# Splitting one input load by tokens and re-dealing the last output stores over three DMA-issuing engines

**Chip, cores, metric.** One core of one Trainium2 chip. The metric is the device time of one execution in microseconds (us), the median of several runs. A DMA has "landed" when the last of its 16 semaphore counts is in the trace.

## The reference, cut to what matters

Linear attention over 8 batches and 8 heads, followed by a two-layer network with SiLU on all 4608 tokens:

```python
q_s, k_s = softmax(q, axis=-1), softmax(k, axis=2)        # (8, 8, 576, 64)
kv = np.einsum('bhsd,bhse->bhde', k_s, v)
x = np.einsum('bhsd,bhde->bhse', q_s, kv)                 # to (4608, 512)
h = x @ w_in                                              # (512, 2048)
return (h * (1 / (1 + np.exp(-h))) @ w_out)               # (2048, 512), float32
```

## The kernel before

The parts that the argument touches. `nc.sync` is SP, `nc.scalar` ACT, `nc.vector` DVE, `nc.gpsimd` GpSimd (POOL in the profile), `nc.tensor` PE (PEld is its weight load). A q behind an engine's name (SPq, POOLq) means its instruction queue. The order of the calls is the order in each engine's queue.

```python
def load(b, name, src, cc, eng):                 # half a batch: 576 KB, one DMA
    t = ld.tile([128, 2, J * D], FP32, name=name)
    st[b][name, cc] = t
    x = src[b].rearrange("(g r) (p j) d -> g (r p) (j d)", r=2, j=J)
    eng.dma_start(out=t, in_=x.rearrange("g x y -> x g y")[:, 2 * cc:2 * cc + 2, :])

def vcast(b, cc, eng, g0=0, g1=2):               # v to bf16, by pairs of heads
    o = vaug[:, :, 2 * cc + g0:2 * cc + g1, 0:D]
    i = jgd(b, "vt", cc)[:, :, g0:g1, :]
    copy(eng, o, i)

# ... the start, batch 0
load(0, "vt", v, 0, nc.sync)
load(0, "kt", k, 1, nc.sync)
load(0, "vt", v, 1, nc.sync)
# ...
xt_mm(0, 0, 320, 256, 0, 0)
heat(3, 6)                                       # three warm-up matmuls of 512 columns
vcast(0, 1, nc.scalar, 0, 1)
vcast(0, 1, nc.vector, 1, 2)
trcopy(0, 1, 0, 5, 2, nc.scalar)
trcopy(0, 1, 5, J, 3)
kv(0, 1)                                         # the k-v product: 36 matmuls, 64 rows
# ... the middle: what is planned for one chunk t, by unit number
for i in range(2):
    # ...
    plan(u + (2, 11)[i], lambda i=i: vcast(b, i, nc.gpsimd))
# ... the end: one tile of the output
def part(name, bank, th, n, a):
    o = w_out_tile(last, th)[:, a, n * HN:(n + 1) * HN]
    nc.vector.scalar_tensor_tensor(out=o, in0=PS[...], scalar=OS, in1=WG[...], ...)
    one, two = {
        (0, 0): (nc.sync, nc.sync),
        (1, 1): (nc.gpsimd, nc.gpsimd),
        (1, 0): (nc.scalar, nc.sync),
        (0, 1): (nc.scalar, nc.gpsimd) if a == 0 else (nc.sync, nc.scalar),
    }[th, n]
    for i, eng in enumerate((one, two)):         # two stores of 64 KB
        eng.dma_start(out=rows(...), in_=o[i * P:(i + 1) * P, :])
```

The softmax here doesn't subtract the row's maximum and nothing guards it: scores larger than these inputs give would overflow.

## Time and profile before

| | |
|---|---|
| time, 3 runs | 263.25 us median (262.77 to 263.55) |
| span of the profiled run | 260.8 us, granted clock 1.000 |
| first wide matmul starts | 15.26 us |
| last arithmetic (DVE) ends | 256.90 us |
| last store lands | 259.62 us |
| from last arithmetic to the end | 3.90 us |

The rows are points on one time axis, from the first to the last instruction. The change works ahead of the second row and behind the fourth. The lines that show this are in the prediction.

### The profile page before, as it was taken

To read this page: it belongs to the slowest core of one execution; us is meant where nothing else is said; L and a number is where in the kernel's file an instruction comes from. 1 tells how busy PE (TensorE), PEld (TensorE's weight loads), DVE (VectorE), ACT (ScalarE), POOL (GpSimd) and SP (SyncE) were. 2 spreads that over 40 slices of the span, in tenths; PEclk is the share of its full clock that TensorE was granted. 3 is DMA by queue.
4 is the path that set the end of the run, shared out by engine and by line. 5 is a ranking of instruction groups with operands and counts; after the bars stand their busy time and mean duration, and the time that the engine had idled before them with its cause. 6 is when DMAs were issued, how large, how long until landed. Compare 5 with 4: busy or idle time off the path is not lost.

```text
span 260.8 us, 6412 instructions
## 1 busy us (share of the span) xinstructions
PE 252.4 (97%) x2732; PEld 203.0 (78%) x2732; DVE 207.3 (79%) x268; ACT 187.6 (72%) x212; POOL 66.9 (26%) x62
## 2 busy tenths in 40 slices
PE   8799999999999999999999999999999999999993
PEld 3457756656887888888888888888888888888882
DVE  2967786879997999799979997999798548855832
ACT  5767877998994799579956996699664757584710
POOL 1753691741360306030603060306000000000004
PEclk9999999999999999999999999999999999999999
DMA  7999999689979477957784879640424002500534
GB/s 248 334 198 298 298 323 333 253 186 384 309 284 222 123 209 247 197 146 201 258 220 118 214 249 152 182 104 3 90 61 102 3 0 46 117 3 1 120 84 121
DMA packets 35452, 45.89 MB, mean 176 GB/s; under 512 B 16208, under 2 KB 19984, under 8 KB 35424
## 3 DMA queue, kind: packets, MB, share of 16 engines
q1 hardware_dynamic: 29488, 33.63, 47.2%
q0 software_dynamic: 5616, 11.60, 16.9%
q8 instruction: 21, 0.34, 0.5%
q10 hardware_dynamic: 320, 0.26, 0.4%
q14 instruction: 7, 0.06, 0.1%
HBM read 36.70 MB, written 9.44 MB: 177 GB/s over the span
## 4 chain that ended last, share of the span: by engine, by line
PE 80%; DVE 12%; ACT 2%; POOL 2%; DMA 1%; issue 1%; POOLq 0%; DVEq 0%; ACTq 0%
PE PS L468 34%; PE PS L368 32%; PE PS L405 5%; PE PS L258 3%; PE PS L228 2%; DVE zq L148 2%; PE PS L189 2%; DVE h L346 2%; DMA qt<-in_q_dram 1%; PE PS L276 1%; DVE eq L157 1%; DVE GT L442 1%; DVE S L442 1%; ACT eq L108 1%; POOL out_dram L730 1%
## 5 line engine op out<-in xcount | busy, mean ns | idle before, releaser
L346 DVE TENSOR_TENSOR h<-PS,h 128x1024 f32<-128x1024 f32 (+1 forms) x45 | 53.9, 1199 | 12.0 <-PE PS L368 6.0
L468 PEld LDWEIGHTS <-GT 128*128 128x128 f16 x512 | 49.5, 98 | 6.9 <-issue 1.2
L368 PEld LDWEIGHTS <-WS 128*128 128x128 f16 x480 | 46.8, 98 | 7.5 <-issue 1.4
L468 PE MATMUL PS<-W,GT 128*128 128x256 f16 x384 | 49.1, 273 | 0.0
L368 PE MATMUL PS<-XS,WS 128*128 128x256 f16 (+1 forms) x360 | 46.3, 272 | 0.6 <-DVE h L346 0.5
L352 ACT ACTIVATE GT<-h 128x1024 f16<-128x1024 f32 (+1 forms) x45 | 46.1, 1047 | 0.3 <-DVE h L346 0.3
L89 ACT COPY h<-PS 128x1024 f32<-128x1024 f32 (+1 forms) x35 | 35.1, 1003 | 13.9 <-PE PS L368 13.4
L157 POOL TENSOR_TENSOR eq<-eq,rzq 128x1152 bf16<-128x1152 bf16 x13 | 27.7, 2134 | 57.6 <-DVE rzq L152 56.1
L468 PEld LDWEIGHTS <-S 128*128 128x128 f16 x384 | 37.1, 98 | 5.5 <-issue 1.0
L368 PEld LDWEIGHTS <-W 128*128 128x128 f16 x360 | 34.7, 98 | 4.8 <-issue 0.5
L468 PE MATMUL PS<-T,S 128*128 128x256 f16 x256 | 32.7, 273 | 0.1
L368 PE MATMUL PS<-XT,W 128*128 128x256 f16 (+1 forms) x240 | 29.5, 272 | 0.1
L352 ACT ACTIVATE GT<-PS 128x1024 f16<-128x1024 f32 (+1 forms) x15 | 15.2, 1016 | 18.9 <-PE PS L368 18.9
L91 POOL CAST vaug<-vt 128x1152 bf16<-128x1152 f32 x12 | 15.8, 1322 | 43.3 <-DMA vt<-in_v_dram 41.1
L730 POOL DMA_DIRECT2D out_dram<-ow x5 | 2.7, 546 | 72.1 <-DVE ow L715 72.1
L108 ACT ACTIVATE eq<-qt 128x1152 bf16<-128x1152 f32 (+1 forms) x18 | 19.0, 1057 | 2.5 <-DMA qt<-in_q_dram 2.4
L113 ACT ACTIVATE ek<-kt 128x1152 bf16<-128x1152 f32 x16 | 18.4, 1153 | 1.2 <-DMA kt<-in_k_dram 1.2
L148 DVE TENSOR_REDUCE zq<-eq 128x18 f32<-128x1152 bf16 x12 | 16.1, 1344 | 3.8 <-ACT eq L108 3.8
L258 PE MATMUL PS<-XT,W 128*128 128x288 f16 x128 | 16.3, 286 | 0.5 <-DVE XT L91 0.2
L468 PE MATMUL PS<-W,S 128*128 128x256 f16 x128 | 16.5, 273 | 0.0
L488 DVE SCALAR_TENSOR_TENSOR ow<-PS,sc 128x512 f32<-128x512 f32 x7 | 4.8, 691 | 14.4 <-ACT sc L484 14.4
L258 PEld LDWEIGHTS <-W 128*128 128x128 f16 x128 | 12.4, 98 | 4.3 <-issue 1.3
(78 smaller groups left out, 346.0 us busy)
## 6 DMA issues: line engine op xcount, KB each, us to landing
out_dram<-ow SPq DMA_DIRECT2D x64, 128.0 KB, 2.4
qt<-in_q_dram SPq DMA_DIRECT2D x12, 576.0 KB, 4.4
kt<-in_k_dram SPq DMA_DIRECT2D x12, 576.0 KB, 5.5
vt<-in_v_dram SPq DMA_DIRECT2D x12, 576.0 KB, 5.4
qt<-in_q_dram POOLq DMA_DIRECT2D x4, 576.0 KB, 10.3
kt<-in_k_dram POOLq DMA_DIRECT2D x4, 576.0 KB, 13.9
vt<-in_v_dram POOLq DMA_DIRECT2D x4, 576.0 KB, 13.2
W<-in_moe_w_out_dram POOLq DMA_DIRECT2D x4, 512.0 KB, 15.0
```

What stands on the lines that cost most here:

```text
L89: eng.copy(out=o, in_=i)
L91: eng.tensor_copy(o, i)
L108: nc.scalar.activation(out=half(st[b]["eq"], cc)[:, :, g0:g1], in_=jgd(b, "qt", cc)[:, :, g0:g1], func=ACT.Exp)
L113: nc.scalar.activation(out=half(ek, cc), in_=jgd(b, "kt", cc), func=ACT.Exp)
L148: nc.vector.reduce_sum(out=z, in_=e, axis=AX.X)
L157: eng.tensor_tensor(out=e, in0=e, in1=r[:, :, :, None].to_broadcast([128, J, 2, D]), op=ALU.mult)
L258: nc.tensor.matmul(out=PS[:, 2 * (fb % 3) + n, 0:S // 2], lhsT=W1[:, c, fb * 128:(fb + 1) * 128], rhs=XTS[0][:, c, n * (S // 2):(n + 1) * ...
L346: nc.vector.tensor_tensor(out=four(t, i), in0=group_bank(t, True), in1=four(t, i), op=ALU.add)
L352: nc.scalar.activation(out=group_out(t, f, n), in_=x, func=ACT.Silu, scale=1.0 / XS)
L368: nc.tensor.matmul(out=PS[:, bank + p // 2, (p % 2) * HT:(p % 2) * HT + width(t)], lhsT=a[:, c, p * 128:(p + 1) * 128], rhs=bb[:, c, 0:wid ...
L405: nc.tensor.matmul(out=PS[:, 2 + tb, :], lhsT=GTS[t % 2][:, fc, tb * 128:(tb + 1) * 128], rhs=W2[:, fc, :], start=(fc == 0), stop=(fc == N ...
L468: nc.tensor.matmul(out=PS[:, bank, m * HN:(m + 1) * HN], lhsT=a[:, fc, m * 128:(m + 1) * 128], rhs=bb[:, fc, :], start=(first and fc == 0) ...
```

## The change

Its intent: (1) the second half of batch 0's v comes in two pieces of tokens, so that one engine can cast the first piece while the second still arrives; (2) no engine issues more than two of the last stores in a row, so that the last ones don't queue up behind an issue.

```diff
-    def load(b, name, src, cc, eng):
+    def load(b, name, src, cc, eng, js=(0, J)):
...
-        eng.dma_start(out=t, in_=x.rearrange("g x y -> x g y")[:, 2 * cc:2 * cc + 2, :])
+        x = x.rearrange("g x y -> x g y")[:, 2 * cc:2 * cc + 2, :]
+        for j0, j1 in zip(js, js[1:]):
+            eng.dma_start(out=t[:, :, j0 * D:j1 * D], in_=x[:, :, j0 * D:j1 * D])
...
-    def vcast(b, cc, eng, g0=0, g1=2):
-        o = vaug[:, :, 2 * cc + g0:2 * cc + g1, 0:D]
-        i = jgd(b, "vt", cc)[:, :, g0:g1, :]
+    def vcast(b, cc, eng, g0=0, g1=2, j0=0, j1=J):
+        o = vaug[:, j0:j1, 2 * cc + g0:2 * cc + g1, 0:D]
+        i = jgd(b, "vt", cc)[:, j0:j1, g0:g1, :]
...
-    load(0, "vt", v, 1, nc.sync)
+    load(0, "vt", v, 1, nc.sync, (0, 5, J))
...
-    vcast(0, 1, nc.scalar, 0, 1)
-    vcast(0, 1, nc.vector, 1, 2)
+    vcast(0, 1, nc.vector, j1=5)
+    vcast(0, 1, nc.scalar, j0=5)
...
-            (0, 0): (nc.sync, nc.sync),
-            (1, 1): (nc.gpsimd, nc.gpsimd),
-            (1, 0): (nc.scalar, nc.sync),
-            (0, 1): (nc.scalar, nc.gpsimd) if a == 0 else (nc.sync, nc.scalar),
-        }[th, n]
+            (0, 0): ((nc.sync, nc.sync), (nc.sync, nc.sync)),
+            (1, 1): ((nc.sync, nc.sync), (nc.gpsimd, nc.gpsimd)),
+            (1, 0): ((nc.scalar, nc.scalar), (nc.gpsimd, nc.gpsimd)),
+            (0, 1): ((nc.sync, nc.scalar), (nc.sync, nc.gpsimd)),
+        }[th, n][a]
```

## The prediction

> **What bounds the kernel now.** I read the busy shares first, then the chain of waits near both edited places, then the timeline of those microseconds, then the DMA records. TensorE carries the kernel:
>
> ```profile
> PE 252.4 (97%) x2732; PEld 203.0 (78%) x2732; DVE 207.3 (79%) x268; ACT 187.6 (72%) x212; POOL 66.9 (26%) x62
> ```
>
> The change touches neither the matmuls nor anything between 15 and 250 us of the 260.8 us span. So the question is two small ones: does the first wide matmul (15.26 us) start earlier, and does the last store land earlier? Here is the chain of waits around the split load of v, then the timeline of the same stretch (start, length, both us):
>
> ```profile
> 12.36 0.44 PE PS L228 x8
> 12.80 0.76 PE PS L542 x3
> 13.55 0.45 PE PS L189 x32
> 14.02 0.18 DVE rz L200
> ...
> 12.65 0.68 ACT L89 CAST vaug<-vt 128x576 bf16<-128x576 f32 x1 [0.16 <-DMA vt<-in_v_dram]
> 12.65 0.76 DVE L91 CAST vaug<-vt 128x576 bf16<-128x576 f32 x1 [0.35 <-DMA vt<-in_v_dram]
> 12.73 0.82 PE L542 MATMUL PS<-XS 128*128 128x512 f16 x3
> 13.48 0.48 PE L189 MATMUL PS<-vaug,ek 64*64 64x65 bf16 x36
> ```
>
> Both casts really wait for the load. But the chain does not run through them: it runs through the three warm-up matmuls of L542 that stand ahead of the k-v product (L189) in TensorE's queue. I test that on the two other places where 64-row products follow 512-column matmuls:
>
> ```profile
> 9.18 1.67 PE L542 MATMUL PS<-XS 128*128 128x512 f16 x7
> 10.78 0.48 PEld L189 LDWEIGHTS <-ek 64*64 64x64 bf16 x36 [0.42 <-issue]
> ...
> 37.73 1.24 PE L405 MATMUL PS<-W,GT 128*128 128x512 f16 x5
> 38.90 0.29 PE L189 MATMUL PS<-vaug,ek 64*64 64x65 bf16 x12
> ```
>
> The product (or its weight load) starts 0.07 us before the recorded end of the last wide matmul in each: 10.85 - 10.78, 38.97 - 38.90, and in our place 13.55 - 13.48. The same offset three times, with different casts behind it, says that our product starts when TensorE lets it, not when the cast ends (13.41). The waits view names ACT vaug as its releaser with 0.4 us; I put that aside as the later of two releases only by the profile's bookkeeping, since the cast on DVE ended later still.
>
> At the end, stores issue from three queues; the last arithmetic is the DVE line:
>
> ```profile
> 254.39 2.70 POOL L730 DMA_DIRECT2D out_dram<-ow  x5 [72.14 <-DVE ow L715]
> 255.18 2.70 ACTq L730 DMA_DIRECT2D out_dram<-ow  x4
> 256.47 0.42 DVE L715 SCALAR_TENSOR_TENSOR ow<-PS,sb 128x256 f32<-128x256 f32 x1 [0.45 <-PE PS L468]
> ...
> 256.67 1.22 ACTq L730 DMA_DIRECT2D out_dram<-ow  x2
> 256.93 0.47 SPq L730 DMA_DIRECT2D out_dram<-ow  x1
> ...
> 257.00:258.00 1.00, 0.00 (x0) 0.00 (x0) 0.00 (x0) 0.00 (x0) 0.09 (x1) 1.00 0.93 242
> 258.00:259.00 1.00, 0.00 (x0) 0.00 (x0) 0.00 (x0) 0.00 (x0) 0.00 (x0) 1.00 0.85 266
> 259.00:260.80 1.80, 0.00 (x0) 0.00 (x0) 0.00 (x0) 0.00 (x0) 0.00 (x0) 1.00 0.02 7
> ```
>
> The data is ready at 256.90; SP issues its half at 256.93, but ACT is still in its third issue and starts the fourth at 257.33 (the trace's single record; it fills the second half of the x2 line). The semaphore counts put that store's landing at 259.62, and the span ends 1.18 us later, after SP has gone through its list of store semaphores (0.06 us each) and the closing barrier. From 256.9 to 260.8 nothing computes; the last table rows (second last column: DMA share) show the DMA engines 0.93 and 0.85 busy until 259, then idle.
>
> **What the skill says.** "DMA: Bandwidth & Descriptors" bears on all of it. Its section on the anatomy of one DMA gives a fixed cost of about 2.0 us, mostly the write receipt; the trace agrees: four 64 KB stores issued alone by SP from 248.69 landed 2.00 to 2.07 us after their issue began, two from POOL 1.97 and 1.98. "Issuing engines are not separate DMA queues" says that dealing out over queues saves only the sequencer's issue time; here that is 0.53 to 0.74 us per issue, and it is what the change can save. "Why small descriptors are slow" gives a fixed cost per packet; here 2304 B packets took 93 ns and 1024 B ones 45 (medians). "Queues, rings and completion order" says that a DMA engine alternates between queues at packet boundaries; no run shows it yet, and it is my main risk.
>
> **Part one, the split load.** One DMA of 576 KB becomes two of 320 and 256 KB. The old one issued from 3.33 to 3.80; the second piece issues by about 4.3, long before the engines reach it, so issue is free. Its packets become 1280 and 1024 B, with the same 16 data packets per engine in each piece. A straight line through the two sizes above is 6.6 ns + 0.0375 ns/B, so 1280 B costs an estimated 54.6 ns. On the slowest engines the load before (k) landed at 11.15 and v at 12.63, which is 1.48 us = 16 x 93 ns. New: 16 x 54.6 = 0.87 and 16 x 45 = 0.72. First piece at about 12.03, second at about 12.75, 0.1 later than the whole used to land.
>
> Casts: DVE is busy with kvn until 12.30, so it starts its 5/9 at 12.32. 640 elements against 576 in 0.756 us are at most 0.84, end 13.16 instead of 13.41. ACT casts 512 elements: full and half casts took 1.16 and 0.68, so 0.84 ns an element, 0.62 us, from 12.77 to 13.40 instead of 13.33. The built program shows that the product's first matmul now waits for DVE alone, and its 21st for ACT. The 36 matmuls start at 8 ns spacing (13.481 to 13.770), so the 21st is due at 13.64, and ACT is done 0.24 before. Everything is ready, and the product still starts at 13.48 behind the warm-up. Sum on the path: 0.0 us. The 0.25 us that DVE gains goes into waiting for the product's end at 14.0, where rz starts. The ACT copy of qT moves from 13.91 to about 13.98; its reader starts at 14.57.
>
> **Part two, the stores.** Still 16 of 64 KB, 5 from POOL; SP goes from 7 to 8 and ACT from 4 to 3. The last two tiles' issues were spread POOL x5, ACT x4, SP x3; now SP x4, POOL x5, ACT x3, in another order. Step by step with ready times from the DVE records (254.09, 254.42, 255.15, 255.48, 256.03, 256.90):
> - SP: 254.12 and 254.65 (formerly POOL from 254.39), then 256.05, then 256.93.
> - ACT: 255.18, 255.79, then 256.55, done by 257.1. It no longer has a fourth.
> - POOL: its first issue began 0.29 us after its data, so 254.72 and 255.27, then 255.84 and 256.37, done at 256.90, and the last at 256.93 to 257.19, depending on whether it pays the 0.29 again.
>
> So the last issue moves from 257.33 to 256.93 on SP and at worst 257.19 on POOL. Landing: the last SP store took 2.48 us before, in a backlog that began in part because two stores of the first pair went out at 254.39 rather than 254.12 and one by one. The four POOL stores under load took 2.0 to 2.5. With 2.1 to 2.3 us I get 259.05 to 259.45, middle 259.25: 0.37 less than 259.62. The shifted semaphores put the last store two or three places from the end of SP's list instead of four: another 0.06 to 0.12. Sum: 0.43, say 0.4.
>
> Total: 0.0 + 0.4, so 263.25 - 0.4 = 262.85. I add a little for the risk below and say 262.9.
>
> **Rivals.**
> - *The split hurts.* In three engines the old v load ended about 0.5 us after the others (landings 12.20, 12.58, 12.63 against 11.96 for the 13th). By then the weight load of the GpSimd queue has packets waiting (first one at 11.09). One v load never let them in between; two loads give the engine a boundary at about 11.5. If one short packet slips in (0.1 to 0.2 us), ACT's cast ends near 13.6 and nothing or 0.05 us is lost. If all 16 descriptors of that weight load slip in (16 x 98 ns = 1.57 us), the cast ends at about 15.0 and the kernel loses about 1.3 us: about 264.2. I give the latter one chance in twelve.
> - *The cast is on the path after all*, if the 0.07 us offset is chance. The product could then start at 13.39 at the earliest (the third warm-up matmul starts at 13.17 and streams 0.216): at most 0.09 us gained, 262.75. For it speaks only the waits view's name.
> - *The end is bound by DMA throughput*, not issue. For it: shares of 0.93 and 0.85, landings 0.2 us apart at the end. Then the last landing hardly moves: 263.2. Against: the twelve stores' packets sum to about 3.0 us of engine time in a stretch of 3.7, so there is slack.
>
> **Range and chances.** The three runs before span 0.8 us, more than the gain. 262.1 to 263.7 holds my 0.4 with that scatter. Two per cent is 5.3 us, which neither part can reach in either direction: faster 0.01, slower 0.01, within 0.98.
>
> **What would show it.** Right: L189 again at about 13.48, 0.07 before the warm-up's end, although the DVE cast ends near 13.16; first wide matmul at 15.26; no issue after 257.2; last landing near 259.25. Wrong: L189 earlier than 13.45 (the cast was on the path); its second part stalled, with ACT idle on DMA vt past 12.9 (the interleave); last landing at 259.5 or later with issues on time (throughput); or anything between 15 and 250 us shifting by more than 0.2 us, which I hold to be untouched.

## The result, and the profile after

| | before | changed |
|---|---|---|
| time, 6 runs each | 263.35 us (262.77 to 263.73) | 264.29 us (263.23 to 264.88) |
| span of the profiled run, clock | 260.8 us, 1.000 | 263.1 us, 0.995 |
| first wide matmul starts | 15.26 | 15.49 |
| last arithmetic ends | 256.90 | 258.28 |
| last store lands, after that | +2.72 | +2.91 |
| end, after that | +3.90 | +4.80 |

The ratio is 1.0038, with a 95% interval of 1.0014 to 1.0063: within 2%, but slower by about 1.0 us, where 0.35 us of gain was predicted. The two profiled runs are unlike in luck: the changed kernel's is among its slowest runs (264.86), the one of before was faster than all six of its timed runs (262.57). So their spans, 2.29 us apart, are not the result, and have to be taken apart.

The line numbers of the changed kernel are higher by two. The page's line of busy shares is as good as unmoved:

```profile
PE 252.3 (96%) x2732; PEld 203.0 (77%) x2732; DVE 207.7 (79%) x268; ACT 187.6 (71%) x212; POOL 65.8 (25%) x62
```

The start, in the timeline of the changed kernel (start, length, engine, line, operation, what it waited for):

```profile
12.50 0.56 DVE L91 CAST vaug<-vt 128x640 bf16<-128x640 f32 x1
12.86 0.82 PE L544 MATMUL PS<-XS 128*128 128x512 f16 x3
13.20 0.62 ACT L89 CAST vaug<-vt 128x512 bf16<-128x512 f32 x1 [0.34 <-DMA vt<-in_v_dram]
13.61 0.58 PE L191 MATMUL PS<-vaug,ek 64*64 64x65 bf16 x36
15.49 4.80 PE L260 MATMUL PS<-XT,W 128*128 128x288 f16 x35 [0.25 <-DVE XT L91]
```

The DVE cast ends at 13.06, and the product (L191) still starts at 13.61, which is 0.07 before the warm-up's recorded end, 13.68. That is the offset of the kernel before.

The end, in its timeline:

```profile
255.51 3.27 SPq L732 DMA_DIRECT2D out_dram<-ow  x4
256.11 2.19 POOL L732 DMA_DIRECT2D out_dram<-ow  x4 [72.47 <-DVE ow L717]
256.57 1.84 ACTq L732 DMA_DIRECT2D out_dram<-ow  x3
257.86 0.42 DVE L717 SCALAR_TENSOR_TENSOR ow<-PS,sb 128x256 f32<-128x256 f32 x1 [0.45 <-PE PS L470]
258.58 0.53 POOL L732 DMA_DIRECT2D out_dram<-ow  x1 [0.28 <-DVE ow L717]
```

The issues are where they were meant to be: ACT is done early, SP starts its last one at 258.31 (a single record, part of its x4), 0.03 after the data, and GpSimd at 258.58. No issue starts later than 0.30 after the data, against 0.43 before. But the last landing is not earlier. The table of stretches of the changed kernel (start and end, length, then the busy time of PE, PEld, DVE, ACT and POOL; second last is the DMA engines' mean share) puts the DMA engines' work up to 260:

```profile
259.00:260.00 1.00, 0.00 (x0) 0.00 (x0) 0.00 (x0) 0.00 (x0) 0.11 (x1) 1.00 0.97 276
260.00:263.10 3.10, 0.00 (x0) 0.00 (x0) 0.00 (x0) 0.00 (x0) 0.00 (x0) 0.57 0.12 40
```

The last store landed at 261.19, yet the program went on for another 1.90 us; before, that was 1.18. What ended last is told by the chain of waits at the end. I had asked for this view of the kernel before ahead of the prediction, and its last line stood there, but the prediction makes no use of it. The kernel before:

```profile
254.97 0.85 POOL out_dram L730 x2
...
256.04 0.53 POOL out_dram L730
256.57 0.52 POOLq L845
```

and the changed kernel:

```profile
257.77 0.53 POOL out_dram L732
258.30 0.26 issue
258.56 0.55 POOLq L847
```

In both the chain ends on POOLq, GpSimd's queue, and not on SP, whose walk through the store semaphores I had taken for the end. The single records behind the last line are a DRAIN of GpSimd's queue. In the changed kernel it is recorded from 258.56 to 262.31; SP had ended its walk at 261.50. Before, the two were level, 260.01 and 260.02, so the times alone could not tell which of them the end waits for. In the changed kernel GpSimd's next record, the step of the closing barrier that the other engines then wait for, starts at 262.35, 0.04 after the drain.

That gives a **theory**: the end is set by whichever is later, SP's walk, or GpSimd's closing drain, and the drain ends about 1.1 us after GpSimd's own last landing, where SP needs only 0.3 to 0.4. Moving the very last store to GpSimd then costs about 0.8 us more than the same landing on SP. (The expectations below call this theory A.) **Rivals**: the split costs it, by a later product or by the load's packets (B); the stores land later because the DMA engines are fuller (C); or the 1 us comes from the middle, since the profiled changed kernel also took 1.16 us longer from its first wide matmul to its last arithmetic (241.64 before, 242.80 after).

### The profile page after: what moved, and what is told of

The parts are those of the page before. It is cut to its first block, busy times and chain, and to the rows that moved or that the text cites. A ratio compares the mean times of both kernels' runs of the same rounds, so it can differ in the third digit from the quotient of the medians.

```text
span 263.1 us, 6410 instructions
## 1 busy us (share of the span) xinstructions
PE 252.3 (96%) x2732; PEld 203.0 (77%) x2732; DVE 207.7 (79%) x268; ACT 187.6 (71%) x212; POOL 65.8 (25%) x62
## 4 chain that ended last, share of the span: by engine, by line
PE 76%; DVE 9%; DMA 5%; issue 4%; POOL 3%; ACT 1%; POOLq 0%; DVEq 0%; ACTq 0%
PE PS L470 33%; PE PS L370 31%; PE PS L407 5%; DMA qt<-in_q_dram 5%; PE PS L230 2%; DVE h L348 2%; PE PS L191 2%; POOL W L547 1%; PE PS L278 1%; DVE GT L444 1%; DVE zq L150 1%; DVE S L444 1%; DVE W L454 1%; POOL out_dram L732 1%; POOL h L128 0%
## 5 line engine op out<-in xcount | busy, mean ns | idle before, releaser
L91 POOL CAST vaug<-vt 128x1152 bf16<-128x1152 f32 x12 | 14.9, 1245 | 43.4 <-DMA vt<-in_v_dram 43.4
```

The source lines that it names most:

```text
L91: eng.tensor_copy(o, i)
```

## The experiments

Twelve runs, one of them of the changed kernel unedited; all gave correct results. Each table gives the time and ratio against the kernel before of the same call, and the tail, from the last arithmetic's end to the span's end, from the run's trace.

### First call: each part alone, and the last store alone

*split_only*: the load and the casts as changed, the stores of before.

> The load and the casts as changed, the last stores as before. Theory A (the loss is in the closing drain of the GpSimd queue, which in the changed kernel starts with the last store and ended 3.2 us after it): time within 0.2 us of before, and from the last DVE store arithmetic to the end of the span 3.9 us as before. Theory B (the split delays the weight stream behind it, whose landings were up to 1.3 us later in the changed kernel's trace): about 1.0 us slower than before, with the landing of batch 1's first q load again past 25.5 us instead of 24.6.

*stores_only*: the stores as changed, load and casts of before (the last hunk of the diff alone).

> The last stores as changed, the load and casts as before. Theory A: 0.8 to 1.0 us slower than before, 4.8 us from the last DVE arithmetic to the end of the span, and GpSimd's closing drain ending about 3.2 us after its last issue ended and later than SP's walk through the store semaphores. Theory B: within 0.2 us of before or faster.

*last_to_pool*: the kernel before with only the very last store moved from ACT to GpSimd.

```diff
-            (0, 1): (nc.scalar, nc.gpsimd) if a == 0 else (nc.sync, nc.scalar),
+            (0, 1): (nc.scalar, nc.gpsimd) if a == 0 else (nc.sync, nc.gpsimd),
```

> Before, with one store moved: the last one, from ACT to GpSimd. Theory A: this alone costs 0.7 to 1.0 us, since the drain starts with that store. Theory C (the changed order of all stores crowds the DMA engines, the last landing is late): about 0, since eleven of twelve stores stay.

*no_pool*: the kernel before with no late store on GpSimd.

```diff
-            (1, 1): (nc.gpsimd, nc.gpsimd),
-            (1, 0): (nc.scalar, nc.sync),
-            (0, 1): (nc.scalar, nc.gpsimd) if a == 0 else (nc.sync, nc.scalar),
+            (1, 1): (nc.sync, nc.scalar),
+            (1, 0): (nc.sync, nc.scalar),
+            (0, 1): (nc.sync, nc.scalar),
```

> Before, with the last twelve stores on SP and ACT in pairs, none on GpSimd. Theory A: no drain at the end, the last two issues start at 256.93 on the time axis of before, their landing sets the end: 0.2 to 0.5 us faster than before, 3.4 to 3.7 us from the last DVE arithmetic to the end. Theory C: about 0 or slower, since the same bytes have to pass.

Measured, 6 runs each; the kernel before beside them took 263.8 us (262.64 to 265.03, 11 runs):

| run | us (range) | ratio (95%) | tail |
|---|---|---|---|
| split_only | 263.46 (262.57 to 263.89) | 0.9993 (0.9962 to 1.0023) | 3.94 |
| stores_only | 264.06 (263.75 to 264.64) | 1.0022 (0.9990 to 1.0053) | 4.78 |
| last_to_pool | 264.15 (263.28 to 265.41) | 1.0025 (0.9991 to 1.0058) | 4.63 |
| no_pool | 263.33 (262.91 to 263.81) | 0.9995 (0.9967 to 1.0023) | 4.03 |

The ratios alone decide little on this chip: each interval is about 0.6% wide, and the effect is under 0.4%. The tails are clear. They are long in the two kernels whose last store is GpSimd's, and near that of before in the others; split_only, the first rival, has neither a longer tail nor a longer time; batch 1's first q load landed at 24.88 in it, not past 25.5 (and at 25.66 in no_pool, where nothing is split). One moved store is enough, although its issue starts at 257.14, only 0.29 after the data. The timeline of last_to_pool:

```profile
254.92 2.75 POOL L730 DMA_DIRECT2D out_dram<-ow  x5
256.42 0.42 DVE L715 SCALAR_TENSOR_TENSOR ow<-PS,sb 128x256 f32<-128x256 f32 x1 [0.45 <-PE PS L468]
```

POOL's fifth record ends at 257.67; its data landed at 259.54, in step with the last store of the other queues (259.56). SP's walk was through at 259.94 and the drain at 260.69. The later landing cannot be the cause here: it is at +2.71, as before (+2.72).

no_pool has no GpSimd landing to wait for, and gained nothing. SP and ACT now have six late issues each and start the last one 0.67 after the data; it landed at +2.70. There the issue is the limit: each of the twelve landed 1.94 to 2.23 us after its issue began, where the last six of the changed kernel took 2.62 to 3.06. SP's walk then took 0.58, more than the 0.27 to 0.40 of the others, since it meets the semaphore of that last store early in its list.

### Second call: give one store back, and the split's parts

*last_on_act*: the changed kernel, with only the very last store given to ACT.

```diff
-            (0, 1): ((nc.sync, nc.scalar), (nc.sync, nc.gpsimd)),
+            (0, 1): ((nc.sync, nc.scalar), (nc.sync, nc.scalar)),
```

> The changed kernel with one store given back: the very last one from GpSimd to ACT. Theory A (the closing drain of GpSimd's queue ends about 3.0 to 3.2 us after its last DMA issue): the tail, from the last DVE arithmetic to the end of the span, falls from 4.8 to 3.9 us, and the time from about 1.0 us over before to within 0.4 of it. Theory C (the new order crowds the DMA engines): tail stays at 4.5 or more.

*pool_four*: the kernel before, with four late stores on GpSimd instead of five, none of them of the last two output tiles.

```diff
-            (0, 1): (nc.scalar, nc.gpsimd) if a == 0 else (nc.sync, nc.scalar),
+            (0, 1): (nc.sync, nc.sync) if a == 0 else (nc.scalar, nc.sync),
```

> Before, with GpSimd's fifth store and ACT's third of the last twelve given to SP. GpSimd's last issue then ends 0.5 us earlier, and ACT is free for the last tile. Theory A with the landing as second limit: tail 3.6 to 3.75 us instead of 3.9, drain over before SP's walk; time 0.0 to 0.3 us below before, hardly above noise. If the drain does not matter and DMA throughput does: tail 3.9.

*casts_only*: the casts by tokens, with the load in one DMA (the `vcast` hunks, without `(0, 5, J)`).

> Before with the casts split by tokens but one load. If the warm-up matmuls ahead of the product bound its start: product again 6.23 us after the first qnorm starts (as in before, the changed kernel and split_only), first wide matmul 8.0 us after it. If the casts bound it: the DVE cast of 640 elements took 0.56 us instead of 0.76 in the changed kernel, so the product starts up to 0.1 us earlier, 6.13. Time within noise of before either way.

*split_heat1*: split_only with one warm-up matmul instead of three ahead of the product.

```diff
-    heat(3, 6)
+    heat(1, 6)
```

> split_only with one warm-up matmul instead of three ahead of the product. If TensorE's queue bounds the product's start: it starts 0.2 to 0.45 us earlier after the first qnorm (5.8 to 6.05 instead of 6.23), then waits at its 21st matmul for ACT's cast, and its end and the first wide matmul stay where they are (8.1 to 8.2 after the qnorm), set by the second piece's landing. If the cast bounds the start: no change at 6.23.

Measured, in 6, 5, 4 and 4 runs; the kernel before took 263.06 us (262.3 to 263.44, 11 runs):

| run | us (range) | ratio (95%) | tail |
|---|---|---|---|
| last_on_act | 263.59 (262.63 to 263.79) | 1.0010 (0.9993 to 1.0027) | 4.17 |
| pool_four | 263.33 (262.82 to 263.56) | 1.0010 (0.9995 to 1.0024) | 3.95 |
| casts_only | 263.51 (263.39 to 264.01) | 1.0022 (1.0006 to 1.0038) | 3.93 |
| split_heat1 | 262.84 (262.54 to 263.35) | 0.9995 (0.9978 to 1.0011) | 3.90 |

last_on_act undoes one store of the changed kernel, and 0.63 us of the tail goes with it. Its timeline:

```profile
255.64 2.18 POOL L732 DMA_DIRECT2D out_dram<-ow  x4 [72.47 <-DVE ow L717]
...
257.39 0.42 DVE L717 SCALAR_TENSOR_TENSOR ow<-PS,sb 128x256 f32<-128x256 f32 x1 [0.45 <-PE PS L470]
```

GpSimd's last issue now ends at 257.82, just when the last arithmetic does; its data landed at 260.13 and the drain ended at 261.20, still 0.25 after SP. The tail is 4.17, not the 3.9 expected: the last hand-out must be earlier still for the drain to be out of the way. pool_four does that: its drain ends 0.45 before SP's walk. But the tail was 3.95, where the expectation had hoped for less than before: SP had three of the last four stores, started its last one 0.77 after the data, and it landed at +2.92.

split_heat1 tests part one of the prediction, that the product starts when the warm-up lets it. Its timeline:

```profile
12.69 0.56 DVE L91 CAST vaug<-vt 128x640 bf16<-128x640 f32 x1 [0.19 <-DMA vt<-in_v_dram]
12.92 0.39 PE L544 MATMUL PS<-XS 128*128 128x512 f16 x1
13.30 0.35 PE L191 MATMUL PS<-vaug,ek 64*64 64x65 bf16 x20
13.35 0.62 ACT L89 CAST vaug<-vt 128x512 bf16<-128x512 f32 x1 [0.30 <-DMA vt<-in_v_dram]
14.03 0.32 PE L191 MATMUL PS<-vaug,ek 64*64 64x65 bf16 x16 [0.37 <-ACT vaug L89]
```

Counted from the start of the first normalization of q on DVE, which takes out the shift between runs, the product starts at 6.23 us in all four traces with the split and three warm-ups (changed, split_only, last_on_act, and after_again of the third call), although their DVE casts end at 5.52 to 5.78. Here it starts at 6.12, 0.05 after a DVE cast that ends later (6.07). So it was the warm-up that held it. But the other 16 matmuls then wait for the second piece: they start at 14.03, 0.05 after the ACT cast, and the product is not done earlier (its last matmul starts at 6.98, against 6.52 to 6.69). The expectation had 5.8 to 6.05 for the product and 8.1 to 8.2 for the first wide matmul; it was 6.12 and 8.46, because the loads were late in this run (the second piece landed 6.15 after that normalization's start, against 5.18 to 5.86 in the four others). So in this trace, with the warm-up out of the way, the second piece ends the product; what a timely one would have given is not shown.

casts_only met neither branch of its expectation. Its product starts at 6.31 after the first normalization of q (the first qnorm of the expectations), 0.05 after the end of a DVE cast that took 0.76 us beside ACT's, not 0.56: here the cast held it, not the warm-up. It is not alone. Of the nine traces with the load in one DMA, the product starts 0.05 us after the cast that its first matmul needs in five (last_to_pool, no_pool, casts_only, cast_behind, both), at 6.27 to 6.66; in four of these v had landed 5.52 to 5.91 after that normalization's start, against 5.20 to 5.46 in the traces that start at 6.22 or 6.23. The timeline of no_pool, the extreme one:

```profile
13.16 0.67 ACT L89 CAST vaug<-vt 128x576 bf16<-128x576 f32 x1 [0.29 <-DMA vt<-in_v_dram]
13.88 0.57 PE L189 MATMUL PS<-vaug,ek 64*64 64x65 bf16 x36 [0.36 <-ACT vaug L89]
```

casts_only is slower by 0.22% with an interval that leaves out 1. Its stretch from the start to the first wide matmul hardly shows it (8.09 us from the first normalization of q, against 8.01 before), nor does its tail. Its trace has the slow order of the race told below; whether that accounts for the timed runs too, no run shows.

### Third call: the result once more, the race in the middle, and a better order

The middle differed between traces by a race. Here the timelines of the kernel before, of the changed kernel:

```profile
64.06 1.22 DVE L452 TENSOR_TENSOR W<-W 128x2048 f16<-128x2048 f16 x1
64.18 2.12 POOL L91 CAST vaug<-vt 128x1152 bf16<-128x1152 f32 x1 [9.03 <-DMA vt<-in_v_dram]
```

```profile
64.61 1.19 POOL L91 CAST vaug<-vt 128x1152 bf16<-128x1152 f32 x1 [8.82 <-DMA vt<-in_v_dram]
64.69 2.17 DVE L454 TENSOR_TENSOR W<-W 128x2048 f16<-128x2048 f16 x1
```

A subtraction on DVE with both inputs in SBUF and a cast on GpSimd, released by a DMA, fall together. In these two traces, whichever starts first takes 1.2 us; the other takes 2.1 to 2.2 and ends 1.02 to 1.07 us after the first has ended (66.30 after 65.28; 66.86 after 65.79). The Trainium skill, "SBUF — State Buffer", section "Who interferes with whom", says this: such a DVE instruction contends with a GpSimd instruction that reads SBUF, and the second to start blocks until the first is done. The traces agree. That a blocked DVE is on the path is supported by the next numbers.

The stretch from the first wide matmul to the last arithmetic follows the order in all fourteen traces but one. DVE first: 241.19 to 241.88 (before, last_to_pool, no_pool, split_heat1, and three of the third call). GpSimd first: 242.39 to 242.80 (changed, split_only, stores_only, last_on_act, pool_four, casts_only). The exception, pool_three, is told below. Kernels with and without either part of the change stand in both groups, so the race is not in the change. after_again and cast_behind test it.

*after_again*: the changed kernel, unedited.

> The changed kernel again, unedited. The first trace of it had a tail of 4.80 us and, in the middle, a DVE subtraction of 2.17 us instead of 1.22 that began just after GpSimd's cast of v. If the tail is a fixed cost: 4.7 to 4.9 again. The 2.17 should come and go with which of the two engines starts first; it is no part of the change. Time 0.7 to 1.2 us over before.

*cast_behind*: the kernel before, with a copy of one element ahead of that cast on GpSimd. It reads what the subtraction writes, so the cast can't start first.

```diff
             plan(u + (16, 17)[i], lambda i=i: qnorm(b, i, nc.gpsimd))
+            if t == 2 and i == 0:
+                plan(u + 2, lambda: nc.gpsimd.tensor_copy(gate, T3[0:1, 0, 0:1]))
             plan(u + (2, 11)[i], lambda i=i: vcast(b, i, nc.gpsimd))
```

> Before, with one GpSimd copy of one element that makes the first cast of batch 3's v wait for the DVE subtraction that it can collide with. If whichever starts first makes the other wait, this removes the slow case: the subtraction takes 1.22 us, the stretch from the first wide matmul to the last DVE arithmetic 241.4 to 241.8 us in this trace (242.4 to 242.8 in the slow case), and the time is 0.2 to 0.6 us below the mean of before, whose runs are a mixture. If the collision is harmless: no change.

*pool_three*: the kernel before, with three early stores on GpSimd and the rest mostly on SP and ACT in turn (in place of the table's entries):

```diff
+            (0, 0): ((nc.sync, nc.sync), (nc.sync, nc.sync)),
+            (1, 1): ((nc.sync, nc.scalar), (nc.gpsimd, nc.gpsimd)),
+            (1, 0): ((nc.sync, nc.scalar), (nc.gpsimd, nc.scalar)),
+            (0, 1): ((nc.sync, nc.scalar), (nc.sync, nc.scalar)),
+        }[th, n][a]
```

> Before, with three early stores on GpSimd (last issue over by -0.5 us of the last DVE arithmetic) and nine of the last twelve on SP and ACT in turn. Drain theory: GpSimd's last landing at +1.5, its drain over at +2.6, off the path. The end is then SP's walk behind the last landing: with one issue per 0.32 us on the two hardware queues together, as in no_pool, last issue at about +0.05 to +0.3, landing 2.05 to 2.4: tail 3.3 to 3.6 us, 0.3 to 0.6 faster than before. If mixed traffic keeps landings at +2.7 whatever the order: tail 3.9.

*both*: cast_behind and pool_three together.

> The two edits together, cast_behind and pool_three: the sum of their gains, 0.5 to 1.0 us below before.

Measured; the kernel before took 263.19 us (262.6 to 263.62, 11 runs):

| run | us (range) | ratio (95%) | tail |
|---|---|---|---|
| after_again | 264.24 (263.45 to 264.38) | 1.0038 (1.0023 to 1.0053) | 4.84 |
| cast_behind | 262.52 (262.10 to 262.94) | 0.9977 (0.9963 to 0.9991) | 3.99 |
| pool_three | 263.29 (262.99 to 263.60) | 1.0006 (0.9992 to 1.0020) | 3.93 |
| both | 262.84 (262.35 to 263.45) | 0.9988 (0.9973 to 1.0004) | 3.91 |

after_again repeats the loss, and its trace happens to have the fast order. That makes it the clean pair for the kernel before: span 261.68 against 260.80. Its first wide matmul starts at 15.30 (15.26 before), the stretch to the last arithmetic is 241.54 (241.64), the tail 4.84 (3.90). The sum is +0.04 - 0.10 + 0.94 = +0.88: all of it is the tail.

cast_behind keeps DVE first, as its timeline shows:

```profile
64.28 1.22 DVE L452 TENSOR_TENSOR W<-W 128x2048 f16<-128x2048 f16 x1
65.56 0.18 POOL L671 CAST gate<-W 1x1 f32<-1x1 f16 x1 [10.19 <-DVE W L452]
65.68 2.25 POOL L91 CAST vaug<-vt 128x1152 bf16<-128x1152 f32 x2
```

The two casts of the x2 line together take 2.25 us, so neither is blocked. The kernel is faster than both kernels of the case: by 0.23% than the one before, and its stretch from wide matmul to last arithmetic is the shortest seen (241.19, one trace).

pool_three frees the end from GpSimd (the drain ends 1.16 before SP's walk), and the tail is still 3.93, above what was expected: ACT's issues took up to 0.8 us, and the last landing came at +2.90. Its trace also shows the race in another place: a second GpSimd cast from 67.70 (2.08 us), then a DVE subtraction at 68.80 that took 2.06, and a long stretch (242.27), although DVE was first at 64.15. both has no lead over cast_behind, where 0.5 to 1.0 us below before had been expected.

### What the closing records say together

From the single records of each trace, us after the last arithmetic's end:

```
run            GpSimd's last   its drain   drain less   last landing   SP's walk   end   end less the
               store landed    ended       landing      of any         ended             later of the two
before             2.00          3.11        1.11          2.72          3.12     3.90       0.79
changed            2.91          4.02        1.11          2.91          3.22     4.80       0.78
split_only         2.05          3.16        1.11          2.74          3.07     3.94       0.78
stores_only        2.88          3.99        1.11          2.88          3.19     4.78       0.79
last_to_pool       2.69          3.85        1.16          2.71          3.10     4.63       0.78
last_on_act        2.31          3.38        1.07          2.85          3.13     4.17       0.79
pool_four          1.67          2.74        1.07          2.92          3.19     3.95       0.76
pool_three         0.98          2.02        1.03          2.90          3.17     3.93       0.76
after_again        2.94          4.05        1.11          2.94          3.26     4.84       0.79
```

In each row the end is 0.76 to 0.79 after the later of the two, and the drain ends 1.03 to 1.16 after GpSimd's own landing, while that landing moves by 2 us. casts_only, split_heat1, cast_behind and both give the same two figures (1.03 or 1.11; 0.76 to 0.78). So the theory holds in all thirteen traces that have late GpSimd stores (twelve kernels). What the drain does in that 1.1 us, no record shows.

## Why the prediction was wrong, and where it was right

**The start, right for the profiled runs.** In the changed kernel the product's start is set by the warm-up: 0.07 before its recorded end, and split_heat1 shows the cause by taking the warm-up away. In the kernel before this held by a margin of 0.10 only: the ACT cast that the first matmul needs ended at 6.08, so the cast would have allowed a start at 6.13 instead of 6.23. In five of nine traces with the load unsplit the cast did set the start, by up to 0.43. So the rival that the cast is on the path, which I had put aside although the waits view named it, is true of some runs. The landings leave no room for packets of the weight load between the two pieces: on the slowest engines k landed at 11.59, the pieces at 12.48 and 13.18, 0.89 and 0.70 later (0.87 and 0.72 predicted). So the large rival of part one fell, though ACT did wait for v past 12.9 (until 13.20), which I had named as its sign; that was the late loads. Two sizes were off without much effect. The DVE cast took 0.56 us, not up to 0.84; it was off the path. And all the loads came 0.4 later in this run, from the first k and v on (8.52 and 10.02, against 8.16 and 9.66), so the ACT cast ended at 13.82, 0.05 after the 21st matmul was due (20 x 8 ns after 13.61 is 13.77). The product's last matmul started 0.39 after its first instead of 0.29, and the wide matmul came 0.10 later in terms of the first normalization of q. In after_again there was no such wait. In the four traces with the split and three warm-ups the first wide matmul comes 8.01 to 8.17 after that normalization's start, in the nine unsplit ones 8.01 to 8.52: neither a gain nor a cost of the split can be told from them, nor from the timed runs.

**The end, wrong.** The step that failed is part two's sum, which let the span end with the last landing and SP's walk: "Sum: 0.43, say 0.4". Term by term, for the tail:
- Issue: right. SP's last began at 0.03 after the data and GpSimd's at 0.29 (0.03 to 0.29 predicted).
- Landing: mis-sized. With "2.1 to 2.3 us" from issue to landing I got -0.37; the last SP and GpSimd stores took 2.71 and 2.62, and the last landing moved from +2.72 to +2.91, which is +0.19. The trace of before had warned of it: its own last seven stores took 2.29 to 3.23. In no kernel did the last landing come before +2.70: in no_pool, pool_four, pool_three and both the last issue was late (0.64 to 0.77 after the data), in the others that store took 2.29 to 2.68 from its issue. The third rival, that the landing hardly moves, described this better than my middle, and its sign came true (+2.91 is 259.81 on the time axis of before, past 259.5, with issues on time). But that it is DMA throughput is not shown: whether GpSimd's stores among the others or the closer issues stretch the landings, no run separates.
- SP's walk: right. From the last landing to its end it took 0.40 before and 0.31 after, -0.09 (-0.06 to -0.12 predicted).
- The drain: missing. SP was done at +3.22, GpSimd's queue at +4.02. This adds 0.80.

The sum is 0.19 - 0.09 + 0.80 = +0.90, which is 4.80 - 3.90, and 0.34% of 263.35 us beside the 0.38% measured. These are single traces, but after_again, whose middle is as fast as that of before, gives +0.94 for the tail. The cause is shown by edits of one store, in the traces' tails (the timed ratios of these edits are within noise): last_to_pool has it without the change's other stores, last_on_act takes most of it away. The Trainium skill could have warned me: "Perfetto Trace Analysis", section "DMA Instruction — SWDGE (GPSIMD)", says that the profile ends such an instruction when its descriptors are made, not when the data has moved. The trace agrees (recorded end 259.11, landing 261.19): an early end of GpSimd's record says nothing of when its queue is done.

**The rest of the 2.29 us between the two profiled runs.** The tail 0.90; the first wide matmul 0.23, of which 0.13 lies before the first normalization of q; 1.16 in the middle, of which 0.40 had come by 58 us and the rest with the race. I had called a shift in the middle a sign of being wrong. It was one, but of the runs, not of the change: after_again lacks it and has the same ratio, 1.0038.

**What stays open.** Why the drain needs 1.1 us; why the loads of the start came 0.4 later in one run; what stretches the late landings; how often the kernel before loses the race in its timed runs (cast_behind's gain is of that size, but only one trace of before was seen); why casts_only was slower.

## What to carry to other kernels

Before moving a store to another engine at the end, ask not only when it is issued and when it lands, but what that engine still does after the landing: here a store on GpSimd had to land 0.7 to 0.8 us before the last one on the other queues to be harmless (0.72 in the kernel before, where drain and walk ended level). Read the chain of waits at the very end first; it had named GpSimd's queue before the change. And when a difference of half a per cent is at stake, look for two engines whose order varies from run to run before comparing two single traces; an added dependence that fixes the order gained 0.23% here, more than the change was meant to bring.

## What the Trainium skill lacked or had wrong

- No page has the closing cost of GpSimd's queue: its DRAIN ended 1.03 to 1.16 us after the landing of its last store, in thirteen traces, and the program 0.76 to 0.79 after the later of drain and SP's walk. It belongs in "Perfetto Trace Analysis", section "Sequencer-only Instruction (DRAIN, etc)", which gives no time; the record of the changed kernel's drain lasted 3.75 us (258.56 to 262.31), so it holds the wait for the landing.
- "DMA: Bandwidth & Descriptors", section "Issuing engines are not separate DMA queues", says that issuing from several engines only saves the sequencer's issue time. The choice of the engine can also set the end of a program: one store from ACT to GpSimd lengthened the tail from 3.90 to 4.63 us with the last landing unmoved (+2.72, +2.71).
- The fixed cost of about 2.0 us on the same page, section "Anatomy of one DMA — SWDGE (gpsimd) path", held for lone stores (1.97 to 2.07 us) and nearly for the twelve that no_pool deals over SP and ACT (1.94 to 2.23). But the last stores of the changed kernel, issued with others and with GpSimd's among them, took 2.62 and 2.71 us: this figure for one DMA does not size such an end.
- "SBUF — State Buffer", "Who interferes with whom", was right; the runs add sizes: DVE 1.22 or 2.17 us, GpSimd's cast 1.2 or 2.1, by which came first.
